# Attention backward: E and G of four key blocks in one tile and one DMA transpose, a four-pack PE step, and one exp unit more per block

## The chip, the cores and the metric

The kernel runs on one core of one Trainium2 chip. The metric is the device time of that core in microseconds (us). The engines are named as in the profile: PE (matrix multiplication), DVE (vector), ACT (activation), POOL, and SP, whose queue issues DMAs. Several runs of a kernel agree within 0.6% for the kernel before.

## The reference

The program is a transformer block and its gradients. Attention has 2048 positions, 32 heads, head size 16:

```
x = A_x;  xn = layernorm(x)
q, k, v = split(xn @ wqkv)                     # 32 heads of 16
p = softmax(q @ k^T * 0.25);  s = (p @ v) @ wo
g = silu(gelu(layernorm(xn) @ w1 + b1) @ w2 + b2)
out = x + s * g
# returned: out and the gradients for x, wqkv, wo, w1, b1, w2, b2
```

Only attention, forward and backward in one loop, changes. It takes some 1940 of 2629 us.

## The kernel before

Attention goes through 16 pairs of heads. A pair has four blocks of 512 queries, a block has 16 steps, one per key block of 128 keys. In step `g` the kernel

- computes scores `s` of the next step and exponentiates them on ACT into `et` (called E);
- computes `d` (the gradient of the probabilities, up to a factor) for two heads, and multiplies it by E on DVE into `gts` (called G);
- accumulates over the keys in `X`, with matmuls called L, E and G below (source: `Lc`, `NAT` with E, `NAT` with G);
- accumulates, for the block before, the gradients of K and V in `Z`. That needs E and G transposed. G is always transposed by DMA. E of half of the units is transposed by DMA (`ek`); for the other half it is computed again in the other orientation (`t`, then an exp into `e`).

The order of one step, and the transposes:

```python
    dma_units = tuple((kc, qb) for kc in range(4) for qb in (2, 3))
    ...
    etp = sb("etp", 3)      # E of four key blocks
    gtp = sb("gtp", 4)      # G of two key blocks
    gbp = sb("gbp", 5)      # G transposed
    ekp = sb("ekp", 5)      # E transposed
    ...                                                       # cut
        first = g % 16 == 1
        emit_t(g)                    # row packs: 32 rows x 128 columns of the PE array
        if not first:
            emit_le(g - 1)           # column packs: 128 rows x 32 columns
        emit_exp_b(g)
        emit_s(g + 1)                # row packs
        emit_d(g)                    # both heads at once, two PSUM buffers in all
        emit_mult(g)
        emit_exp_a(g + 1)
        emit_dmat(g)
        if first:
            emit_le(g - 1)
        emit_g(g - 1)                # column packs
        emit_z(g - lagb, 0)
        emit_z(g - lagb, 1)

    def emit_dmat(g):
        ...                                                   # cut
        if kb % 2 == 1:              # two transposes of G, 0.5 MB each, per group of four steps
            nc.sync.dma_start_transpose(out=blk[j]["Gk"][kc][:, h], in_=st_gt[g][:].rearrange("k a h q -> k (a h q)"))
        if kb % 4 == 3:              # and one of E, 0.5 MB
            nc.sync.dma_start_transpose(out=ek[:].rearrange("q b m k -> q (b m) k"), in_=st_et[g][:, 2:4].rearrange("k b a h q -> k (b a h q)"))
```

Matmuls on different rows, or on different columns, of the PE array run at the same time, four of them here (the timeline of PE below shows four on columns starting within 0.01 us; at 1200.85 us of the same kernel four on rows do so too): this is what "four-pack" means. On POOL a background task (the slope of gelu) runs along; its loads and stores, and the loads of the next pair's operands, are issued by SP as well.

## Time and profile before

| | before |
|---|---|
| time, median of the first 3 runs | 2628.93 us |
| attention | 282 to 2224 us of the span |
| one block, steady | 29.5 us |
| group of four steps, steady | 7.0 us |
| mean granted PE clock | 0.962 |

The first lines are from the page of the kernel before: busy time and share of the span by engine, the granted clock in 40 slices (tenths of full speed), and the chain of work that ended last, by engine and by line.

```profile
PE 2295.2 (87%) x18152; PEld 731.6 (28%) x18192; DVE 1837.6 (70%) x3286; ACT 1673.4 (64%) x1910; POOL 908.0 (35%) x1391
...
PEclk8899799999999999999999999999999999789999
...
PE 38%; DVE 33%; issue 12%; DMA 10%; ACT 4%; POOL 2%; SPq 0%; ACTq 0%; DVEq 0%; POOLq 0%
...
L743 DVE TENSOR_TENSOR gts<-d,et 128x512 bf16<-128x512 f32 x2048 | 1302.5, 682 | 359.1 <-issue 240.8
...
L708 PE MATMUL d<-QDT,KVT 32*128 32x512 bf16 x2048 | 599.1, 383 | 130.9 <-DVE gts L743 129.5
```

No engine is full, and `d` waits 129.5 us for DVE to finish with its buffers. The timeline of PE shows how (columns: start, duration, engine, line, operation, operands, count, and in brackets the idle time before and what ended it).

```profile
1171.99 0.38 PE L774 MATMUL X<-et,Lc 128*32 128x512 bf16 x2
1172.00 0.38 PE L858 MATMUL Z<-gk,W 128*32 128x512 bf16 x2
1172.22 0.38 PE L777 MATMUL X<-et,NAT 128*32 128x512 bf16 x2
1172.53 0.39 PE L694 MATMUL s<-QDT,KVT 32*128 32x512 bf16 x2
1172.71 0.37 PE L708 MATMUL d<-QDT,KVT 32*128 32x512 bf16 x1
1173.31 0.37 PE L708 MATMUL d<-QDT,KVT 32*128 32x512 bf16 x1 [0.23 <-DVE gts L743]
```

Four matmuls of one pack start within 0.01 us, packs of the same kind follow at 0.215 to 0.23 us, and a change between columns and rows costs a pitch of 0.32 us (1172.22 to 1172.53). The second `d` stands until the second gts of the step before has freed its buffer, and no other matmul starts in between (1172.71 to 1173.31).

The busy time by window gives the load of attention (columns: window, length, PE, weight loads, DVE, ACT, POOL with counts, granted clock, DMA share, GB/s).

```profile
300.00:2200.00 1900.00, 1750.78 (x15400) 472.20 (x15396) 1529.79 (x2592) 1479.56 (x1572) 764.74 (x1241) 0.99 1.17 233
```

### The profile page before, as it was taken

How to read it: one execution, taken by the hardware profiler on the slowest of the kernel's cores; microseconds unless marked ns; L12 is line 12 of the kernel's file. 1: busy time of each engine (PE TensorE's matmuls, PEld its weight loads, DVE VectorE, ACT ScalarE, POOL GpSimd, SP SyncE). 2: the span in 40 equal slices, each digit the busy share in tenths (PEclk: the TensorE clock that was granted, in tenths of full speed). 3: DMA queues.
4: the chain of work that ended last, by engine and by line, in shares of the span. 5: the costliest groups of instructions: out<-in, count | busy, mean ns of one | idle time of the engine just before them, and what ended most of it. 6: DMA issues, size and time to landing. Idle time of an engine off the chain costs nothing.

```text
span 2624.7 us, 47762 instructions
## 1 busy us (share of the span) xinstructions
PE 2295.2 (87%) x18152; PEld 731.6 (28%) x18192; DVE 1837.6 (70%) x3286; ACT 1673.4 (64%) x1910; POOL 908.0 (35%) x1391
## 2 busy tenths in 40 slices
PE   3788699999999999999999899999999997479998
PEld 2333122222222222222222222222222222134446
DVE  5766578887778878788878778888888885201652
ACT  3344578777777877788777777777777775011141
POOL 0533545454535445454445454521101111100020
PEclk8899799999999999999999999999999999789999
DMA  5355899999999999999999999999999998987475
GB/s 192 92 184 184 179 239 232 236 236 234 226 236 237 237 231 237 231 234 242 231 235 233 237 228 240 235 236 233 226 233 229 236 218 183 271 215 186 153 160 125
DMA packets 1905432, 568.51 MB, mean 217 GB/s; under 512 B 1811889, under 2 KB 1887794, under 8 KB 1905202
## 3 DMA queue, kind: packets, MB, share of 16 engines
q1 hardware_dynamic: 1844674, 511.05, 95.8%
q10 hardware_dynamic: 60528, 54.41, 6.7%
q8 instruction: 142, 2.33, 0.4%
q14 instruction: 88, 0.72, 0.1%
HBM read 52.83 MB, written 62.66 MB: 44 GB/s over the span
## 4 chain that ended last, share of the span: by engine, by line
PE 38%; DVE 33%; issue 12%; DMA 10%; ACT 4%; POOL 2%; SPq 0%; ACTq 0%; DVEq 0%; POOLq 0%
DVE gts L743 26%; PE d L708 6%; PE X L789 6%; PE Z L858 4%; DMA gk<-gts 4%; PE Z L852 3%; PE t L680 3%; PE X L774 2%; PE ps_dhg L463 2%; DVE xs L795 2%; ACT et L722 2%; DVE xt L807 2%; PE XT L805 1%; PE ps_dw L528 1%; PE ps_dw L442 1%
## 5 line engine op out<-in xcount | busy, mean ns | idle before, releaser
L743 DVE TENSOR_TENSOR gts<-d,et 128x512 bf16<-128x512 f32 x2048 | 1302.5, 682 | 359.1 <-issue 240.8
L722 ACT ACTIVATE et<-s 128x1024 bf16<-128x1024 f32 x1024 | 1002.6, 1024 | 24.9 <-PE d L708 13.8
L730 ACT ACTIVATE e<-t 128x1024 bf16<-128x1024 f32 x512 | 523.8, 1023 | 407.3 <-PE t L680 405.7
L708 PE MATMUL d<-QDT,KVT 32*128 32x512 bf16 x2048 | 599.1, 383 | 130.9 <-DVE gts L743 129.5
L694 PE MATMUL s<-QDT,KVT 32*128 32x512 bf16 x2048 | 403.3, 390 | 18.2 <-DMA QDT<-QDPad 11.9
L774 PE MATMUL X<-et,Lc 128*32 128x512 bf16 x2048 | 403.9, 391 | 14.1 <-DVE xs L795 14.1
L777 PE MATMUL X<-et,NAT 128*32 128x512 bf16 x2048 | 403.9, 391 | 0.0
L789 PE MATMUL X<-gts,NAT 128*17 128x512 bf16 x2048 | 402.5, 389 | 0.0
L858 PE MATMUL Z<-gk,W 128*32 128x512 bf16 x2048 | 399.4, 384 | 0.0
L822 POOL TENSOR_TENSOR W<-NATQd,rL 128x128 bf16<-128x128 bf16 x64 | 25.7, 402 | 645.9 <-DVE rL L817 645.9
L789 PEld LDWEIGHTS <-NAT 128*17 128x17 bf16 x2048 | 92.5, 87 | 492.0 <-issue 492.0
L852 PE MATMUL Z<-e,W 128*32 128x512 bf16 x1024 | 202.2, 388 | 3.8 <-DVE acc L865 2.3
L852 PE MATMUL Z<-ek,W 128*32 128x512 bf16 x1024 | 203.7, 394 | 0.0
L680 PE MATMUL t<-KVT,QDT 32*128 32x512 bf16 x1024 | 201.0, 389 | 0.0
L694 PEld LDWEIGHTS <-KVT 32*128 32x128 bf16 x2048 | 97.4, 91 | 362.6 <-issue 362.5
L708 PEld LDWEIGHTS <-KVT 32*128 32x128 bf16 x2048 | 139.0, 91 | 88.9 <-issue 59.6
L774 PEld LDWEIGHTS <-Lc 128*32 128x32 bf16 x2048 | 103.7, 93 | 180.4 <-issue 179.4
L865 DVE TENSOR_TENSOR acc<-Z,acc 64x512 f32<-64x512 f32 x192 | 129.2, 673 | 12.2 <-PE Z L858 12.2
L852 PEld LDWEIGHTS <-W 128*32 128x32 bf16 x2048 | 121.1, 93 | 56.7 <-issue 50.2
L777 PEld LDWEIGHTS <-NAT 128*32 128x32 bf16 x2048 | 101.2, 96 | 52.2 <-issue 2.7
L631 POOL TENSOR_TENSOR bg_v<-bg_t 128x512 f32<-128x512 f32 x56 | 58.1, 1038 | 149.1 <-ACT bg_t L638 149.1
L870 POOL CAST ob<-acc 64x512 bf16<-64x512 f32 x64 | 38.6, 603 | 203.3 <-DVE acc L865 203.3
(161 smaller groups left out, 2525.8 us busy)
## 6 DMA issues: line engine op xcount, KB each, us to landing
gk<-gts SPq DMA_TRANSPOSE x512, 4.1
HGT_s<-hgT SPq DMA_DIRECT2D x2, 3584.0 KB, 12.2
bg_x<-H1T_s SPq DMA_DIRECT2D x56, 128.0 KB, 2.8
GP_s<-bg_m SPq DMA_DIRECT2D x56, 128.0 KB, 2.5
gp<-GP_s ACTq DMA_DIRECT2D x8, 896.0 KB, 8.5
DH1T_s<-dh1T SPq DMA_DIRECT2D x4, 1792.0 KB, 10.2
NAT<-NAT_s SPq DMA_DIRECT2D x16, 264.0 KB, 3.2
GB_s<-gB ACTq DMA_DIRECT2D x16, 256.0 KB, 2.0
```

The costliest lines, as they stand in the source:

```text
L680: nc.tensor.matmul(t[:, hj, :], lhsT=op["QDT"][r:r + 32, q0:q0 + 128], rhs=op["KVT"][r:r + 32, kc * 512:(kc + 1) * 512], start=True, stop= ...
L694: nc.tensor.matmul(s[:, hj, :], lhsT=op["KVT"][r:r + 32, kb * 128:(kb + 1) * 128], rhs=op["QDT"][r:r + 32, qc * 512:(qc + 1) * 512], start ...
L708: nc.tensor.matmul(d[:], lhsT=op["KVT"][r:r + 32, kb * 128:(kb + 1) * 128], rhs=op["QDT"][r:r + 32, qc * 512:(qc + 1) * 512], start=True, ...
L722: nc.scalar.activation(out=et[:, :, kb % 4, :, :].rearrange("k b h q -> k h b q"), in_=st_s.pop(g)[:].rearrange("k h (b q) -> k h b q", b= ...
L730: nc.scalar.activation(out=e[:], in_=st_t.pop(g)[:], func=ACT.Exp)
L743: nc.vector.tensor_tensor(out=gts[:, kb % 2, hj, :].rearrange("k (b q) -> k b q", b=4), in0=ds[hj][:].rearrange("k (b q) -> k b q", b=4), ...
L774: nc.tensor.matmul(X[64 + 32 * hj:96 + 32 * hj, :], lhsT=Lc[:], rhs=et[:, :, kb % 4, hj, :], start=(kb == 0), stop=False, skip_group_check ...
L777: nc.tensor.matmul(X[32 * hj:32 * hj + 32, :], lhsT=NATt[:, kb, hj, 1:33], rhs=et[:, :, kb % 4, hj, :], start=(kb == 0), stop=(kb == 15), ...
L789: nc.tensor.matmul(X[64 + 32 * hj:64 + 32 * hj + 17, :], lhsT=NATt[:, kb, hj, 0:17], rhs=gts[:, kb % 2, hj, :], start=False, stop=(kb == 1 ...
L852: nc.tensor.matmul(Z[32 * hj:32 * hj + 32, :], lhsT=blk[j]["W1"][:, qb, hj, :], rhs=ev[:, hj], start=(qb == qb_order[0]), stop=False, tile ...
L858: nc.tensor.matmul(Z[32 * hj:32 * hj + 32, :], lhsT=blk[j]["W2"][:, qb, hj, :], rhs=gv[:, :, :, hj, qb, :], start=False, stop=(qb == qb_or ...
L865: nc.vector.tensor_tensor(out=av, in0=Z[0:64, :], in1=av, op=ALU.add)
```

## The change

Its intent: take PE out from behind DVE by issuing the two `d` of a step half a step apart; fill every pack to three or four matmuls; let SP issue one large transpose per group instead of three; move plain DMAs from SP to ACT; and relieve DMA by computing one more unit of E again (the exp unit: `t` and `e`), so that the first group of a block moves 1.25 MB instead of 1.5. `xs` moves from DVE to ACT.

```diff
-    dma_units = tuple((kc, qb) for kc in range(4) for qb in (2, 3))
+    n_moved = (1, 2, 2, 2)
+    dma_units = tuple((kc, qb) for kc in range(4) for qb in range(4 - n_moved[kc], 4))
@@ pools
-    etp = sb("etp", 3)
-    gtp = sb("gtp", 4)
-    gbp = sb("gbp", 5)
-    ekp = sb("ekp", 5)
-    ep = sb("ep", lagb + 2)
+    egp = sb("egp", 3)
+    tgp = sb("tgp", 5)
+    ep = sb("ep", 4)
@@ operand loads; the two transfers of the gelu slope likewise
-            nc.sync.dma_start(out=t["NAT"][:]...
+            nc.scalar.dma_start(out=t["NAT"][:]...
@@ emit_exp_a: one tile for E and G
+            eg = egp.tile([128, 8192], bf16, name="eg")
@@ emit_dmat, once per four steps
+        n = n_moved[kc]
+        tg = tgp.tile([128, 48, 128], bf16, name="tg")
+        nc.sync.dma_start_transpose(out=tg[:, 0:8 * n + 32, :], in_=st_et[g][0][:, (4 - n) * 1024:8192])
@@ emit_zg: odd units go to the upper half of Z, so two units make a four-pack
+            c = 32 * hj + 64 * (i % 2)
@@ the step
+        emit_s(g + 1)
+        emit_d(g, 0)
+        if not first:
+            emit_l(g - 1)
+        if i == 0:
+            emit_e(g - 1)
+        else:
+            emit_ze(gz)
+            if i % 2 == 1:
+                emit_zg(gz - 1)
+                emit_zg(gz)
+        emit_d(g, 1)
+        emit_t(g)
         ...                                                  # cut: exps, mult, acc, dmat
+        if i != 0:
+            emit_e(g - 1)
         emit_g(g - 1)
+        if i == 0:
+            emit_ze(gz)
```

(The copies for the operands share one padded tile; `acc` has 128 partitions, and its upper half is added on POOL at the end of a pair.)

More of the change, by code (lines that the diff above doesn't have):

```diff
@@ L569, in attention_core @@
         ))
-    KVPad = opnd.tile([128, 16, 4, 32], bf16, name="KVPad")
-    QDPad = opnd.tile([128, 16, 4, 32], bf16, name="QDPad")
-    nc.gpsimd.memset(KVPad[:], 0.0)
-    nc.gpsimd.memset(QDPad[:], 0.0)
+    Pad = opnd.tile([128, 16, 4, 32], bf16, name="Pad")
+    nc.gpsimd.memset(Pad[:], 0.0)
     Lc = opnd.tile([128, 32], bf16, name="Lc")
@@ L577, in attention_core @@
     opnd.tile([128, 192], mybir.dt.uint8, name="pad_to_256b")
-    acc = opnd.tile([64, S], f32, name="acc")
+    acc = opnd.tile([128, S], f32, name="acc")
     def load_ops(p):
@@ L583, in plain @@
         def plain():
-            nc.sync.dma_start(out=t["NAT"][:].rearrange("q k j c -> q k (j c)"), in_=NAT_s[p])
-            nc.sync.dma_start(out=t["NATQq"][:].rearrange("q k j c -> q k (j c)"), in_=NATQ_s[0][p])
-            nc.sync.dma_start(out=t["NATQd"][:].rearrange("q k j c -> q k (j c)"), in_=NATQ_s[1][p])
+            nc.scalar.dma_start(out=t["NAT"][:].rearrange("q k j c -> q k (j c)"), in_=NAT_s[p])
+            nc.scalar.dma_start(out=t["NATQq"][:].rearrange("q k j c -> q k (j c)"), in_=NATQ_s[0][p])
+            nc.scalar.dma_start(out=t["NATQd"][:].rearrange("q k j c -> q k (j c)"), in_=NATQ_s[1][p])
         def ck():
-            nc.gpsimd.tensor_copy(out=KVPad[:, :, 0:2, 0:17], in_=t["NAT"][:, :, :, 0:17])
-            nc.gpsimd.tensor_copy(out=KVPad[:, :, 2:4, 0:16], in_=t["NAT"][:, :, :, 17:33])
+            nc.gpsimd.tensor_copy(out=Pad[:, :, 0:2, 0:17], in_=t["NAT"][:, :, :, 0:17])
+            nc.gpsimd.tensor_copy(out=Pad[:, :, 2:4, 0:16], in_=t["NAT"][:, :, :, 17:33])
         def tk():
             nc.sync.dma_start_transpose(out=t["KVT"][:].rearrange("r (m k) -> r m k", m=16),
-                                        in_=KVPad[:].rearrange("q m j c -> q (m j c)"))
+                                        in_=Pad[:].rearrange("q m j c -> q (m j c)"))
         def cq():
-            nc.gpsimd.tensor_copy(out=QDPad[:, :, 0:2, 0:17], in_=t["NATQq"][:])
-            nc.gpsimd.tensor_copy(out=QDPad[:, :, 2:4, 0:16], in_=t["NATQd"][:])
+            nc.gpsimd.tensor_copy(out=Pad[:, :, 0:2, 0:17], in_=t["NATQq"][:])
+            nc.gpsimd.tensor_copy(out=Pad[:, :, 2:4, 0:16], in_=t["NATQd"][:])
         def tq():
             nc.sync.dma_start_transpose(out=t["QDT"][:].rearrange("r (m k) -> r m k", m=16),
-                                        in_=QDPad[:].rearrange("q m j c -> q (m j c)"))
-        return [plain, ck, cq, tk, tq]
+                                        in_=Pad[:].rearrange("q m j c -> q (m j c)"))
+        return [plain, ck, tk, cq, tq]
     blocks = [(p, qc) for p in range(npairs) for qc in range(nqc)]
@@ L607, in attention_core @@
     NSTEP = NB * 16
-    st_s, st_t, st_d, st_et, st_e, st_gt = {}, {}, {}, {}, {}, {}
+    st_s, st_t, st_d, st_et, st_e = {}, {}, {}, {}, {}
     blk = [dict(Gk={}, Ek={}) for _ in range(NB)]
@@ L614, in attention_core @@
     GC = float(np.sqrt(2.0 / np.pi))
+    n_slope = 4 * FC
     def gelu_slope_ops():
@@ L619, in load @@
             x = bgp.tile([128, 512], bf16, name="bg_x")
-            nc.sync.dma_start(out=x[:], in_=H1T_s[fc * 128:(fc + 1) * 128, sc * 512:(sc + 1) * 512])
+            nc.scalar.dma_start(out=x[:], in_=H1T_s[fc * 128:(fc + 1) * 128, sc * 512:(sc + 1) * 512])
             return x
@@ L623, in gelu_slope_ops @@
         yield
-        for i in range(4 * FC):
+        for i in range(n_slope):
             sc, fc = divmod(i, FC)
@@ L641, in gelu_slope_ops @@
             tt(m, m, x)
-            if i + 1 < 4 * FC:
+            if i + 1 < n_slope:
                 nx = load(i + 1)
@@ L654, in gelu_slope_ops @@
             yield
-            nc.sync.dma_start(out=GP_s[fc * 128:(fc + 1) * 128, sc * 512:(sc + 1) * 512], in_=m[:])
+            yield
+            nc.scalar.dma_start(out=GP_s[fc * 128:(fc + 1) * 128, sc * 512:(sc + 1) * 512], in_=m[:])
             yield
@@ L695, in emit_s, with emit_d @@
                              start=True, stop=True, tile_position=(r, 0))
-    def emit_d(g):
+    def emit_d(g, hj):
         a = a_unit(g)
@@ L703, in emit_d @@
         qc = blocks[j][1]
-        ds = []
-        for hj in range(2):
-            r = 64 + 32 * hj
-            d = ps_d.tile([128, 512], f32, name="d", tag="d")
-            nc.tensor.matmul(d[:], lhsT=op["KVT"][r:r + 32, kb * 128:(kb + 1) * 128], rhs=op["QDT"][r:r + 32, qc * 512:(qc + 1) * 512],
-                             start=True, stop=True, tile_position=(r, 0))
-            ds.append(d)
-        st_d[g] = ds
+        r = 64 + 32 * hj
+        d = ps_d.tile([128, 512], f32, name="d", tag="d")
+        nc.tensor.matmul(d[:], lhsT=op["KVT"][r:r + 32, kb * 128:(kb + 1) * 128], rhs=op["QDT"][r:r + 32, qc * 512:(qc + 1) * 512],
+                         start=True, stop=True, tile_position=(r, 0))
+        st_d.setdefault(g, []).append(d)
     def emit_exp_a(g):
@@ L718, in emit_exp_a @@
         if kb % 4 == 0:
-            cur["et"] = etp.tile([128, 4, 4, 2, 128], bf16, name="et")
-        et = cur["et"]
-        st_et[g] = et
-        nc.scalar.activation(out=et[:, :, kb % 4, :, :].rearrange("k b h q -> k h b q"),
+            eg = egp.tile([128, 8192], bf16, name="eg")
+            cur["eg"] = (eg, eg[:, 0:4096].rearrange("k (b a h q) -> k b a h q", b=4, a=4, h=2),
+                         eg[:, 4096:8192].rearrange("k (a h q) -> k a h q", a=4, h=2))
+        st_et[g] = cur["eg"]
+        nc.scalar.activation(out=cur["eg"][1][:, :, kb % 4, :, :].rearrange("k b h q -> k h b q"),
                              in_=st_s.pop(g)[:].rearrange("k h (b q) -> k h b q", b=4), func=ACT.Exp)
@@ L736, in emit_mult @@
         kb = a[1]
-        if kb % 2 == 0:
-            cur["gts"] = gtp.tile([128, 2, 2, 512], bf16, name="gts")
-        gts = cur["gts"]
-        st_gt[g] = gts
+        _, et, gts = st_et[g]
         ds = st_d.pop(g)
         for hj in range(2):
-            nc.vector.tensor_tensor(out=gts[:, kb % 2, hj, :].rearrange("k (b q) -> k b q", b=4), in0=ds[hj][:].rearrange("k (b q) -> k b q", b=4),
-                                    in1=st_et[g][:, :, kb % 4, hj, :], op=ALU.mult)
+            nc.vector.tensor_tensor(out=gts[:, kb % 4, hj, :].rearrange("k (b q) -> k b q", b=4), in0=ds[hj][:].rearrange("k (b q) -> k b q", b=4),
+                                    in1=et[:, :, kb % 4, hj, :], op=ALU.mult)
     def emit_dmat(g):
         a = a_unit(g)
-        if a is None:
+        if a is None or a[1] % 4 != 3:
             return
@@ L751, in emit_dmat, with emit_l @@
         kc = kb // 4
-        if kb % 2 == 1:
-            h = (kb // 2) % 2
-            if h == 0:
-                blk[j]["Gk"][kc] = gbp.tile([128, 2, 16, 128], bf16, name="gk")
-            nc.sync.dma_start_transpose(out=blk[j]["Gk"][kc][:, h], in_=st_gt[g][:].rearrange("k a h q -> k (a h q)"))
-        if kb % 4 == 3:
-            ek = ekp.tile([128, 2, 8, 128], bf16, name="ek")
-            for qb in (2, 3):
-                blk[j]["Ek"][(kc, qb)] = ek[:, qb - 2]
-            nc.sync.dma_start_transpose(out=ek[:].rearrange("q b m k -> q (b m) k"), in_=st_et[g][:, 2:4].rearrange("k b a h q -> k (b a h q)"))
-    def emit_le(g):
+        n = n_moved[kc]
+        tg = tgp.tile([128, 48, 128], bf16, name="tg")
+        nc.sync.dma_start_transpose(out=tg[:, 0:8 * n + 32, :], in_=st_et[g][0][:, (4 - n) * 1024:8192])
+        for i in range(n):
+            blk[j]["Ek"][(kc, 4 - n + i)] = tg[:, 8 * i:8 * i + 8]
+        blk[j]["Gk"][kc] = tg[:, 8 * n:8 * n + 32]
+    def emit_l(g):
         a = a_unit(g)
@@ L770, in emit_le @@
         X = blk[j]["X"]
-        NATt = op_of(j)["NAT"]
-        et = st_et[g]
+        et = st_et[g][1]
         for hj in range(2):
@@ L775, in emit_le, with emit_e @@
                              start=(kb == 0), stop=False, skip_group_check=True, tile_position=(0, 64 + 32 * hj))
+    def emit_e(g):
+        a = a_unit(g)
+        if a is None:
+            return
+        j, kb = a
+        X = blk[j]["X"]
+        NATt = op_of(j)["NAT"]
+        et = st_et[g][1]
         for hj in range(2):
@@ L786, in emit_g @@
         NATt = op_of(j)["NAT"]
-        gts = st_gt[g]
+        gts = st_et[g][2]
         for hj in range(2):
-            nc.tensor.matmul(X[64 + 32 * hj:64 + 32 * hj + 17, :], lhsT=NATt[:, kb, hj, 0:17], rhs=gts[:, kb % 2, hj, :],
+            nc.tensor.matmul(X[64 + 32 * hj:64 + 32 * hj + 17, :], lhsT=NATt[:, kb, hj, 0:17], rhs=gts[:, kb % 4, hj, :],
                              start=False, stop=(kb == 15), skip_group_check=True, tile_position=(0, 64 + 32 * hj))
         st_et.pop(g)
-        st_gt.pop(g)
         if kb == 15:
             xs = xsp.tile([128, 512], f32, name="xs")
-            nc.vector.tensor_copy(out=xs[:], in_=X[:])
+            nc.scalar.copy(out=xs[:], in_=X[:])
             blk[j]["xs"] = xs
@@ L805, in emit_finalize @@
             nc.tensor.transpose(XT[:, qb, :], xs[:, qb * 128:(qb + 1) * 128], ident_f32[:])
-        xt = finp.tile([128, 4, 128], f32, name="xt")
+        xt = finp.tile([128, 4, 128], f32, name="xt", bufs=1)
         nc.vector.tensor_copy(out=xt[:], in_=XT[:])
@@ L835, in emit_finalize, with z_unit @@
         blk[j]["W2"] = W2
-    def emit_z(g, part):
+    def z_unit(g):
         b = b_unit(g)
         if b is None:
-            return
-        j, kc, qb = b
-        p, qc = blocks[j]
-        if part == 0:
-            if qb == qb_order[0]:
-                cur["Z"] = ps_z.tile([64, 512], f32, name="Z", tag="z")
-            Z = cur["Z"]
-            if (kc, qb) in dma_units:
-                ev = blk[j]["Ek"].pop((kc, qb)).rearrange("q (a h) k -> q h a k", h=2)
-            else:
-                ev = st_e.pop(g)[:].rearrange("q h (a k) -> q h a k", a=4)
-            for hj in range(2):
-                nc.tensor.matmul(Z[32 * hj:32 * hj + 32, :], lhsT=blk[j]["W1"][:, qb, hj, :], rhs=ev[:, hj],
-                                 start=(qb == qb_order[0]), stop=False, tile_position=(0, 32 * hj))
-            return
-        Z = cur["Z"]
-        gv = blk[j]["Gk"][kc][:].rearrange("q a (r h b) k -> q a r h b k", r=2, h=2)
-        for hj in range(2):
-            nc.tensor.matmul(Z[32 * hj:32 * hj + 32, :], lhsT=blk[j]["W2"][:, qb, hj, :], rhs=gv[:, :, :, hj, qb, :],
-                             start=False, stop=(qb == qb_order[3]), tile_position=(0, 32 * hj))
-        if qb == qb_order[3]:
-            av = acc[:, kc * 512:(kc + 1) * 512]
-            if qc == 0:
-                nc.vector.tensor_copy(out=av, in_=Z[0:64, :])
-            else:
-                nc.vector.tensor_tensor(out=av, in0=Z[0:64, :], in1=av, op=ALU.add)
-            if qc == nqc - 1:
-                if kc == 0:
-                    cur["ob"] = outp.tile([64, S], bf16, name="ob")
-                ob = cur["ob"]
-                nc.gpsimd.tensor_copy(out=ob[:, kc * 512:(kc + 1) * 512], in_=av)
-                if kc == 3:
-                    for hj in range(2):
-                        for kv in range(2):
-                            late.append((g + lagb + 2, lambda hj=hj, kv=kv: nc.sync.dma_start(
-                                out=dKVT_out[(1 - kv) * D + p * 32 + hj * 16:(1 - kv) * D + p * 32 + hj * 16 + 16, :],
-                                in_=ob[hj * 32 + kv * 16:hj * 32 + kv * 16 + 16, :])))
@@ new lines, in z_unit, with emit_ze @@
+            return None
+        return b + (g % 4,)
+    def emit_ze(g):
+        u = z_unit(g)
+        if u is None:
+            return
+        j, kc, qb, i = u
+        if i == 0:
+            cur["Z"] = ps_z.tile([128, 512], f32, name="Z", tag="z")
+        Z = cur["Z"]
+        if (kc, qb) in dma_units:
+            ev = blk[j]["Ek"].pop((kc, qb)).rearrange("q (a h) k -> q h a k", h=2)
+        else:
+            ev = st_e.pop(g)[:].rearrange("q h (a k) -> q h a k", a=4)
+        for hj in range(2):
+            nc.tensor.matmul(Z[32 * hj:32 * hj + 32, :], lhsT=blk[j]["W1"][:, qb, hj, :], rhs=ev[:, hj],
+                             start=(i == 0), stop=False, tile_position=(0, 32 * hj), skip_group_check=True)
@@ new lines, in emit_zg, with emit_acc @@
+    def emit_zg(g):
+        u = z_unit(g)
+        if u is None:
+            return
+        j, kc, qb, i = u
+        Z = cur["Z"]
+        gv = blk[j]["Gk"][kc].rearrange("q (a h b) k -> q a h b k", a=4, h=2)
+        for hj in range(2):
+            c = 32 * hj + 64 * (i % 2)
+            nc.tensor.matmul(Z[c:c + 32, :], lhsT=blk[j]["W2"][:, qb, hj, :], rhs=gv[:, :, hj, qb, :],
+                             start=(i == 1), stop=(i >= 2), tile_position=(0, c), skip_group_check=True)
+    def emit_acc(g):
+        u = z_unit(g)
+        if u is None or u[3] != 3:
+            return
+        j, kc, qb, i = u
+        p, qc = blocks[j]
+        Z = cur["Z"]
+        av = acc[:, kc * 512:(kc + 1) * 512]
+        if qc == 0:
+            nc.vector.tensor_copy(out=av, in_=Z[:])
+        else:
+            nc.vector.tensor_tensor(out=av, in0=Z[:], in1=av, op=ALU.add)
+        if qc == nqc - 1:
+            if kc == 0:
+                cur["ob"] = outp.tile([64, S], bf16, name="ob")
+            ob = cur["ob"]
+            hi = outp.tile([64, 512], f32, name="hi")
+            nc.gpsimd.tensor_copy(out=hi[:], in_=acc[64:128, kc * 512:(kc + 1) * 512])
+            nc.gpsimd.tensor_tensor(out=ob[:, kc * 512:(kc + 1) * 512], in0=acc[0:64, kc * 512:(kc + 1) * 512],
+                                    in1=hi[:], op=ALU.add)
+            if kc == 3:
+                for hj in range(2):
+                    for kv in range(2):
+                        late.append((g + lagb + 2, lambda hj=hj, kv=kv: nc.sync.dma_start(
+                            out=dKVT_out[(1 - kv) * D + p * 32 + hj * 16:(1 - kv) * D + p * 32 + hj * 16 + 16, :],
+                            in_=ob[hj * 32 + kv * 16:hj * 32 + kv * 16 + 16, :])))
@@ L894, in attention_core @@
         first = g % 16 == 1
+        gz = g - lagb
+        i = gz % 4
+        emit_s(g + 1)
[4 more added lines that the diff above has]
+            emit_e(g - 1)
+        else:
+            emit_ze(gz)
[3 more added lines that the diff above has]
+        emit_d(g, 1)
         emit_t(g)
-        if not first:
-            emit_le(g - 1)
+        emit_exp_a(g + 1)
         emit_exp_b(g)
-        emit_s(g + 1)
-        emit_d(g)
         emit_mult(g)
-        emit_exp_a(g + 1)
+        emit_acc(gz)
         emit_dmat(g)
         if first:
-            emit_le(g - 1)
+            emit_l(g - 1)
+        if i != 0:
+            emit_e(g - 1)
         emit_g(g - 1)
-        emit_z(g - lagb, 0)
-        emit_z(g - lagb, 1)
+        if i == 0:
+            emit_ze(gz)
         if g >= 17 and (g - 17) % 16 == 0 and (g - 17) // 16 < NB:
```

## The prediction

> **What bounds it now.** Attention, about 281 to 2224 us, is most of the span; only it changes. There (busy time by window) PE is busy 92%, DVE 81%, ACT 78%: nothing is full. The timeline shows a fixed rhythm of 7.0 us per four steps, 29.5 us per block of 16 (xs copy to xs copy). It is a PE-DVE loop. Both d matmuls of a step are issued together into two buffers. Every second step PE waits for the second gts to free its buffer (d at 1202.12, next d at 1202.71), then for acc before Z (1203.02, then 1203.30). DVE meanwhile idles 0.57 to 0.85 us. The chain of waits agrees: PE 38%, DVE 33%, gts alone 26%. Without those waits PE needs about 5.2 us per four steps.
>
> DMA is not the bound: binning the packets gives a plateau of 290 GB/s, the mean is 234.[...]
>
> **What changes, with durations of the trace.**
> - PE: same packs of matmuls (4.5 per step, 0.215 us each), but four row/column changes per step instead of three. A change makes the pitch 0.32 instead of 0.215[...]. Cost: 0.05 us per step. In return d is split: head 0 at the step's start, head 1 half a step later with t, so PE no longer stands behind two gts; Z's first write moves to the end of its step, after acc.
> - DVE: loses xs (0.68 us per block). gts (pitch 0.605) and acc stay.
> - ACT: one exp more (pitch 0.92), xs (about 0.6), 2.5 DMA issues per block (0.33 to 0.8 us elsewhere in this trace, partly hidden). About 24 to 25 us per block.
> - DMA: 5.75 instead of 6 MB per block, one issue instead of three. At 290 GB/s about 22 us per block with the rest. A 1.5 MB transpose lands about 7.5 us after issue (estimate); its eg buffer is wanted about 10.5 us after: tight, not binding.
>
> **On the critical path.** I walked the new order by hand with these durations and the two-buffer rings of s/t and d (on the old order the walk gives 3.35 and 3.64 us per two steps, as the timeline shows). Ordinary group: 6.06 us (was 7.0). First group of a block, with the extra exp, xs, transposes of X and finalize: about 8.2. Block: 3 x 6.06 + 8.2 = 26.4; tanh, DMA issues on ACT and jitter make it about 27.0. Saving 2.5 us x 64 = 160 us.
>
> **Predicted: 2470 us, 80% range 2405 to 2555.** Faster by over 2%: 0.89; within 2%: 0.08; slower: 0.03.
>
> **Right or wrong in the profile.** Right: four steps take 6.0 to 6.3 us; d waits for gts mostly gone; PE idle shrinks; ACT and DVE both 87 to 92% busy in attention; DMA mean about 250 GB/s; chain shifts from gts towards et and e. Wrong: et or gts waiting on tg (DMA), long ACT issue times, or d still waiting for gts in most steps.
>
> **What would break it.** The single late transpose may miss its buffer's reuse, so that ACT waits once per group (back towards 2550 or above).[...] d1 and t may not overlap as assumed. The block's first group, with the exp and xs now on the fullest engine, may cost more than 8.2 us.

The sum: a block of 3 x 6.06 + 8.2 = 26.4 us, about 27.0 with what is added, 2.5 us less in each of 64 blocks, 160 us less than 2630, so 2470 us. The 7.5 us for a 1.5 MB transpose: the trace of the kernel before gives about as much, 7.7 us: 4.1 to landing for 0.5 MB and 3.6 for another 1 MB at 290 GB/s (an estimate from these two).

## The result and the profile after

| | before | changed |
|---|---|---|
| median (range), 4 runs each | 2629.94 us (2627.68 to 2637.29) | 2565.49 us (2552.27 to 2573.38) |
| ratio, 95% interval | | 0.9745 (0.9699 to 0.9792) |
| mean granted PE clock of the profiled run | 0.962 | 0.891 |
| steady group of four steps at full clock | 7.0 us | 6.02 us |
| block wholly at full clock, median | 29.55 us (55 of 63) | 26.27 us (33 of 63) |
| time at half clock between first and last step | 64 us | 433 us |

Blocks are counted from the first `s` of a block to that of the next. The trace records the granted clock as stretches at full or at half speed; the last two rows combine those with the steps.

The page of the changed kernel, in the same order as above:

```profile
PE 2324.2 (90%) x18320; PEld 744.8 (29%) x18320; DVE 1853.6 (72%) x3222; ACT 1773.9 (69%) x2038; POOL 990.2 (39%) x1454
...
PEclk8899569888999979699998988698997998889999
...
PE 62%; DMA 15%; ACT 8%; DVE 6%; POOL 3%; SPq 3%; issue 2%; ACTq 1%; DVEq 0%; POOLq 0%
...
L738 DVE TENSOR_TENSOR eg<-d,eg 128x512 bf16<-128x512 f32 x2048 | 1349.4, 687 | 249.4 <-PE d L706 77.6
...
L706 PE MATMUL d<-QDT,KVT 32*128 32x512 bf16 x2048 | 857.4, 419 | 8.8 <-DVE eg L738 8.3
...
L764 PE MATMUL X<-eg,Lc 128*32 128x512 bf16 x2048 | 439.6, 426 | 3.8
```

The wait of `d` for DVE is gone: 129.5 us became 8.3 us. But the mean of one matmul rose (`d` from 383 to 419 ns), and the clock row, all nines in attention before but for its start, now shows many slices of 5 to 8. PE is busier because its matmuls are slower. PE's share of the chain rises from 38% to 62%, in part for the same reason (in E12, where the clock is held, it is 51%) and in part because DVE has left the chain.

Two windows of the changed kernel, 16 and 36 us long, make it plain:

```profile
1180.00:1196.00 16.00, 15.38 (x148) 4.13 (x145) 14.26 (x23) 13.20 (x14) 10.09 (x16) 1.00 1.18 248
910.00:946.00 36.00, 36.00 (x227) 7.07 (x225) 22.49 (x34) 24.40 (x26) 13.49 (x17) 0.50 0.98 212
```

In the second PE is busy 36.00 of 36.00 us and does 6.3 matmuls per us; in the first it is busy 96% and does 9.3. At half clock a step takes 2.47 us (mean of 157), at full clock 1.65 (mean of 828). So 433 us at half clock cost about 433 x (1 - 1.65 / 2.47) = 144 us, an estimate from the trace. Without them the profiled run would be near 2430 us. The repeats point the same way: the four runs had granted clocks of 0.891, 0.895, 0.899 and 0.907, and took 2573.38, 2568.42, 2562.55 and 2552.27 us, in that order. From the first to the last the clock means about 86 us less at half clock (561 to 474 us of the whole span) and the time is 21 us shorter, 0.24 us for each, somewhat less than the third that the estimate takes (E11's fastest and slowest run below: 269 and 78 us, 0.29).

What starts such a stretch? Here is the timeline at 903 us, the second block of a pair, where ACT issues the operand loads (three lines of ACT, then PE):

```profile
903.23 2.22 ACTq L582 DMA_DIRECT2D NATQq<-NATQq_s  x1
...
905.48 1.05 ACTq L583 DMA_DIRECT2D NATQd<-NATQd_s  x1
...
906.58 1.02 ACT L720 ACTIVATE eg<-s 128x1024 bf16<-128x1024 f32 x1 [2.48 <-issue]
...
907.65 0.39 PE L694 MATMUL s<-QDT,KVT 32*128 32x512 bf16 x2 [2.31 <-ACT eg L720]
...
909.48 0.59 PE L694 MATMUL s<-QDT,KVT 32*128 32x512 bf16 x2 [0.20 <-ACT eg L720]
```

ACT stands 2.22 and 1.05 us in issuing; the next exp starts 2.48 us late; PE pauses 2.31 us; and 1.8 us later each matmul takes 0.59 us instead of 0.39. This stretch at half clock lasts 37.5 us, to step 3 of the next block. Why these two issues take so long is not shown. SP is issuing a transpose at the same time, but that alone does not do it: of the 112 issues for the gelu slope on ACT, 99 lie wholly within an issue of SP, and all 112 took 0.33 to 0.37 us. Only the second and the third of three loads in a row took long, and not in every pair. The other kind of start has a late transpose behind it:

```profile
836.27 1.03 ACT L728 ACTIVATE e<-t 128x1024 bf16<-128x1024 f32 x1
838.82 1.94 ACT L720 ACTIVATE eg<-s 128x1024 bf16<-128x1024 f32 x2 [1.52 <-DMA tg<-eg]
```

Here ACT waits 1.52 us to write E, until DMA has read the `eg` tile. In all, 19 stretches at half clock lie between the first blocks and the end of attention, each begins 0.9 to 4.2 us after the start of a PE pause of 0.55 to 2.64 us (the one just shown has 0.55), and seven are over 20 us long. One pause, of 1.64 us at 1260.5 us, has no stretch behind it.

The trace was then cut into the windows of 3.413 us in which the clock changes (every stretch is a multiple of that), from the first step to the last. For each window I took the share of the time in which at least one matmul streams, counting for each the pitch that matmuls of its kind have in this trace when they follow each other: 216 ns for one of 512 columns at full clock (L442, 182 of 221) and 427 at half (L409, 14 of 24), and for one of the 128-column transposes `XT` (L803) 109 and 213; this is an estimate from the pitches.

| window of the changed kernel, attention | number | streaming share, lowest / median / highest |
|---|---|---|
| full clock, stays full | 398 | 0.47 / 0.72 / 0.77 |
| full clock, next is half | 19 | 0.13 / 0.44 / 0.55 |
| half clock, stays half | 106 | 0.54 / 0.80 / 0.84 |
| half clock, next is full | 20 | 0.80 / 0.83 / 0.86 |

In this trace no window with a share above 0.56 came before a fall; between 0.47 and 0.56 some did and some did not. A window before a return is denser in the median (0.83 against 0.80), but the two ranges overlap from 0.80 to 0.84, so this share does not tell when the clock comes back. What can be said: at half clock the new step's windows are about 0.80 full, since each of its four row/column changes takes a pitch of 0.54 us (940.25 to 940.79 us), of which the count takes 0.427 as streaming; it stays at half clock although in 101 of the 106 windows the profile shows under 0.1 us of PE idle; and all seven stretches over 20 us end at step 3 or 4 of the next block, where `XT` and more `t` are.

The kernel before is a useful contrast. It too has 14 PE pauses over 0.8 us in attention after its first block (19 us in sum; the changed kernel has 20, 31 us). Eight stretches at half clock follow after its first blocks, but they last 3.4 to 13.7 us, 41 us in all; the 19 of the changed kernel last 3.4 to 44.4 us, 355 us in all. So the loss is less in the number of pauses than in how long the new order then stays at half clock. Which property of the order does it was not isolated.

### The profile page after: what moved, and what is told of

It reads as the page before. It is cut to its first block, busy times and chain, and to the rows that moved or that the text cites. A ratio compares the mean times of both kernels' runs of the same rounds, so it can differ in the third digit from the quotient of the medians.

```text
span 2571.6 us, 47302 instructions
## 1 busy us (share of the span) xinstructions
PE 2324.2 (90%) x18320; PEld 744.8 (29%) x18320; DVE 1853.6 (72%) x3222; ACT 1773.9 (69%) x2038; POOL 990.2 (39%) x1454
## 4 chain that ended last, share of the span: by engine, by line
PE 62%; DMA 15%; ACT 8%; DVE 6%; POOL 3%; SPq 3%; issue 2%; ACTq 1%; DVEq 0%; POOLq 0%
PE d L706 12%; PE X L764 11%; PE s L694 10%; DMA tg<-eg 9%; PE X L776 7%; PE Z L866 4%; ACT eg L720 3%; PE X L788 3%; ACT e L728 2%; PE ps_dhg L463 2%; PE Z L854 2%; PE ps_h L212 1%; PE ps_dw L442 1%; PE XT L803 1%; PE ps_dw L528 1%
## 5 line engine op out<-in xcount | busy, mean ns | idle before, releaser
L738 DVE TENSOR_TENSOR eg<-d,eg 128x512 bf16<-128x512 f32 x2048 | 1349.4, 687 | 249.4 <-PE d L706 77.6
L720 ACT ACTIVATE eg<-s 128x1024 bf16<-128x1024 f32 x1024 | 1033.2, 1027 | 208.8 <-PE d L706 114.4
L706 PE MATMUL d<-QDT,KVT 32*128 32x512 bf16 x2048 | 857.4, 419 | 8.8 <-DVE eg L738 8.3
L728 ACT ACTIVATE e<-t 128x1024 bf16<-128x1024 f32 x576 | 593.4, 1030 | 79.6 <-PE t L680 78.7
L764 PE MATMUL X<-eg,Lc 128*32 128x512 bf16 x2048 | 439.6, 426 | 3.8
L776 PE MATMUL X<-eg,NAT 128*32 128x512 bf16 x2048 | 440.2, 427 | 0.0
L788 PE MATMUL X<-eg,NAT 128*17 128x512 bf16 x2048 | 434.2, 420 | 0.0
L706 PEld LDWEIGHTS <-KVT 32*128 32x128 bf16 x2048 | 187.9, 92 | 382.1 <-issue 382.1
L866 PE MATMUL Z<-tg,W 128*32 128x512 bf16 x2048 | 222.2, 417 | 0.0
L694 PEld LDWEIGHTS <-KVT 32*128 32x128 bf16 x2048 | 108.1, 92 | 308.7 <-issue 308.0
L854 PE MATMUL Z<-tg,W 128*32 128x512 bf16 x896 | 191.1, 423 | 0.0
L880 DVE TENSOR_TENSOR acc<-Z,acc 128x512 f32<-128x512 f32 x192 | 130.5, 680 | 9.2 <-PE Z L866 9.2
```

What stands on the lines that cost most here:

```text
L694: nc.tensor.matmul(s[:, hj, :], lhsT=op["KVT"][r:r + 32, kb * 128:(kb + 1) * 128], rhs=op["QDT"][r:r + 32, qc * 512:(qc + 1) * 512], start ...
L706: nc.tensor.matmul(d[:], lhsT=op["KVT"][r:r + 32, kb * 128:(kb + 1) * 128], rhs=op["QDT"][r:r + 32, qc * 512:(qc + 1) * 512], start=True, ...
L720: nc.scalar.activation(out=cur["eg"][1][:, :, kb % 4, :, :].rearrange("k b h q -> k h b q"), in_=st_s.pop(g)[:].rearrange("k h (b q) -> k ...
L728: nc.scalar.activation(out=e[:], in_=st_t.pop(g)[:], func=ACT.Exp)
L738: nc.vector.tensor_tensor(out=gts[:, kb % 4, hj, :].rearrange("k (b q) -> k b q", b=4), in0=ds[hj][:].rearrange("k (b q) -> k b q", b=4), ...
L764: nc.tensor.matmul(X[64 + 32 * hj:96 + 32 * hj, :], lhsT=Lc[:], rhs=et[:, :, kb % 4, hj, :], start=(kb == 0), stop=False, skip_group_check ...
```

## The experiments

Two theories stood. CLOCK: the loop is as fast as predicted, and what is missing against the prediction is time at half clock, started by PE pauses and (the part that stays argued) held by the step's own gaps. QUEUE: the waiting itself, for transposes and for DMA issue, is the loss, and the clock is a side effect. A third name, SUPPLY, was added in the second round for the question where the pauses come from: SP and DMA need nearly all of a block's time. All results were correct. Times are medians of four runs, ratios against the runs of the kernel before in the same rounds. "Pauses" are PE idle times over 0.8 us in attention after its first block; "half" is time at half clock between the first and the last step; both are of the profiled run.

### E1: the order of the step alone

```diff
 # the changed kernel, with E and G in tiles of their own (etp 3, gtp 4, gbp 5, ekp 5),
 # three 0.5 MB transposes per group as before, all plain DMAs on SP, and
-    n_moved = (1, 2, 2, 2)
+    n_moved = (2, 2, 2, 2)
```

> One part alone: the new order of the PE step (with xs on ACT and Z in two halves), but E and G in tiles of their own, three 0.5 MB transposes per group, all plain DMAs on SP and no extra exp, as before. Theory CLOCK (the new order removes the d-waits-for-gts loop; what was lost against the prediction is half-clock time started by PE pauses): groups of four steps at full clock still near 6.0 us, blocks wholly at full clock near 26; SP has more to issue (about 25.5 us of transposes and plain DMAs per block), so pauses and half-clock stretches at least as many as in the change's run (433 us); time 2520 to 2600. Rival QUEUE (the gain comes from the merged transposes and the freed SP queue): time close to before, 2600 to 2640.

Measured: 2685.3 us, ratio 1.0204 (1.0175 to 1.0233). Half 644 us, pauses 29, blocks wholly at full clock 26.25 us in the median, but only 18 of 63. The block time is as CLOCK had it; the total is worse than either theory allowed. The new order alone makes the kernel slower than before: it asks for a transpose group every 6 us, the supply cannot follow (gts waits for a transpose to free its buffer 65 times, 97 us in all, against 17 times and 30 us before), and pauses and half clock eat more than the order gains.

### E2: the rest without the order of the step

```diff
 # the changed kernel, with the step in the old order:
+        emit_t(g)
+        if not first:
+            emit_l(g - 1)
+            emit_e(g - 1)
+        emit_exp_b(g)
+        emit_s(g + 1)
+        emit_d(g, 0)
+        emit_d(g, 1)
+        emit_mult(g)
+        emit_exp_a(g + 1)
+        emit_dmat(g)
         ...                          # G, Z with E, Z with G, acc, as before
```

> The other part alone: one merged transpose per group, plain DMAs on ACT, the extra exp, xs on ACT, but the old order of the step. CLOCK: the old rhythm of 7.0 us per ordinary group stays, blocks 29 to 30.5 us, half-clock time within 20 to 150 us[...]; time 2610 to 2660. QUEUE: 2540 to 2590.

Measured: 2606.66 us, ratio 0.9890 (0.9868 to 0.9911). Half 57 us, pauses 4, blocks at full clock 29.44 us. The old rhythm is there as expected; the time is 3 us below the range given, with fewer disturbed blocks than before (58 of 63 are wholly at full clock, against 55). So neither part alone brings the gain. The order makes a faster loop, the merged transposes feed it.

### E3: operand loads back on SP

```diff
-            nc.scalar.dma_start(out=t["NAT"][:]...      # and NATQq, NATQd
+            nc.sync.dma_start(out=t["NAT"][:]...
```

> The change with only the three operand loads of each head pair back on SP. In the change's run ACT stood up to 2.3 us in issuing them (1.84 us for one), and PE paused 1.5 to 2.3 us at step 3 of the second block of a pair, where five of the stretches of 37 to 41 us at half clock begin. CLOCK: those pauses and those stretches go, half-clock time falls from 433 to 150 to 280 us, time 2495 to 2535; pauses in the third block of a pair (late transposes) stay or grow a little. QUEUE: only the 2 us per pair come back, at most 32 us: 2530 to 2555, half-clock time then explains nothing.

Measured: 2526.52 us, ratio 0.9592 (0.9537 to 0.9646). Half 268 us. No stretch begins at step 3 of the second block of a pair any more (in the changed kernel four did, after pauses of 2.12 to 2.64 us). Three DMA issues per pair, 48 in all, on the wrong engine cost some 39 us (2565.49 to 2526.52, two sets of rounds). By the intervals of the two ratios that is 20 to 60 us, so the time alone does not rule out the 32 us that QUEUE allowed at most; the 165 us less at half clock speak for CLOCK. Pauses are still 19, now mostly of the late-transpose kind.

### E4: bursts of empty matmuls, with a flaw

```diff
+    Zc = opnd.tile([128, 32], bf16, name="Zc")           # zeros
+    nc.gpsimd.memset(Zc[:], 0.0)
     Lc = opnd.tile([128, 32], bf16, name="Lc")
@@ before emit_g(g - 1)
+        if g % 16 == 8 and (g // 16) % 4 in (1, 2):
+            for r in range(6):                           # adds zero to X
+                nc.tensor.matmul(X[96:128, :], lhsT=Zc[:], rhs=et[:, :, kb % 4, 1, :], start=False, stop=False, ...)
```

> The change with six extra matmuls with zero weights, adding zero into X, in a row at step 8 of the second and third block of each pair (32 bursts; at most 1.3 us each at full clock, 41 us in all). In the change's run a stretch at half clock ended only at steps 1 to 4 of the next block[...]. CLOCK: stretches that begin in steps 1 to 7 of those blocks now end at step 8 to 10; none of 30 us or more that spans step 8 of such a block is left; half-clock time falls from 433 to 200 to 300 us; time 2520 to 2570 in spite of the added work. QUEUE: the added work simply adds: 2580 to 2605, half-clock stretches as long as before.

Measured: 2778.59 us, ratio 1.0556. This says nothing about the bursts: every block was slower, also those without one, and a transpose took 7.34 us in the median instead of 6.12. The tile of zeros is 64 bytes per partition and had moved every later tile by 64 bytes. That is 20% more time for the same bytes; with the tiles where they were, E5 has 6.14 us again. Why the offset costs time is not shown.

### E5: the same bursts, nothing moved

```diff
-    opnd.tile([128, 192], mybir.dt.uint8, name="pad_to_256b")
+    opnd.tile([128, 128], mybir.dt.uint8, name="pad_to_256b")
```

> The last run again with its flaw mended: its 64-byte tile of zeros had moved every later tile by 64 bytes, and the transposes took 7.34 us each instead of 6.12. Now the zeros lie in the padding and nothing moves. CLOCK: transposes 6.1 us again; half-clock stretches that reach step 8 of the second or third block of a pair end at steps 8 to 10; at most one stretch of over 30 us is left (7 over 20 us in the change's run); half-clock time 200 to 320 us; time 2515 to 2570 in spite of up to 41 us of added work. QUEUE: 2575 to 2605 and stretches as long as before.

Measured: 2530.51 us, ratio 0.9610 (0.9573 to 0.9646). Half 180 us, transposes 6.14 us, pauses 15. Half is below the range given. PE got 192 matmuls more, the blocks that hold them take 27.5 to 30.9 us at full clock (median 28.0) instead of 26.3, and the kernel is 35 us faster. Each of the seven stretches that reach a burst ends within 4 us of its first matmul; here is one, begun 17 us earlier at a pause:

```profile
567.71 0.64 PE L877 MATMUL Z<-tg,W 128*32 128x512 bf16 x4
568.29 0.60 PE L708 MATMUL d<-QDT,KVT 32*128 32x512 bf16 x1
568.29 0.60 PE L682 MATMUL t<-KVT,QDT 32*128 32x512 bf16 x2
568.82 0.61 PE L778 MATMUL X<-eg,NAT 128*32 128x512 bf16 x2
568.83 1.46 PE L787 MATMUL X<-eg,Zc 128*32 128x512 bf16 x3
569.66 0.60 PE L799 MATMUL X<-eg,NAT 128*17 128x512 bf16 x1
570.09 1.49 PE L787 MATMUL X<-eg,Zc 128*32 128x512 bf16 x3
...
572.42 0.39 PE L766 MATMUL X<-eg,Lc 128*32 128x512 bf16 x2
```

Before the burst a matmul takes 0.60 to 0.64 us, after it 0.39. QUEUE expected the added work simply to add, 2580 us or more; it falls. That the half clock is the loss (433 us became 180), and that a dense run of matmuls ends it (seven stretches of seven), is shown by this run. That the step's own gaps are what holds it fits, but is argued: what makes the clock fall or come back is not shown.

### E6: operands spread over the pair

```diff
 # on E3: copies and transposes of the next pair's operands at steps 5, 13, 21, 33 instead of 5, 9, 13, 17
-        return [plain, ck, tk, cq, tq]
+        return [(1, plain), (5, ck), (13, tk), (21, cq), (33, tq)]
```

> Operand loads back on SP, and the copies and transposes of the next pair's operands spread over the second, third and fourth block (steps 5, 13, 21, 33 after its start instead of 5, 9, 13, 17), so that SP's extra 6.5 us per pair do not fall into one stretch. The bytes stay. SUPPLY (SP and DMA need about 25.4 us of each 26.3 us block: a burst makes the merged transposes late, ACT waits for its eg tile, PE pauses, the clock halves): PE pauses over 0.8 us fall from 19 to 8 or fewer, half-clock time from 268 to under 130 us (some 35 of it at the start), time 2450 to 2490. If the pauses came from something else than SP's bursts: unchanged, 2510 to 2545.

Measured: 2515.25 us (2490.46 to 2521.03), ratio 0.9535 (0.9485 to 0.9584). Half 270 us, pauses 13. A miss, and not clear of E3 by the intervals. It does not rule out the bursts of SP, though: in the trace each of the 13 pauses that remain has, in the 20 us before it, either an operand transpose (5) or the loads and stores at the turn of a pair, which were not spread (8).

### E7: one exp unit more, 5.5 MB per block

```diff
 # on E3
-    n_moved = (1, 2, 2, 2)
+    n_moved = (1, 2, 1, 2)
```

> Operand loads back on SP and one exp unit more (the third group of a block moves 1.25 MB too): SP needs 1 us less per block, ACT 0.92 us more. SUPPLY: lateness and pauses fall, half-clock time under 150 us; a block at full clock grows by 0.3 to 0.6 us (26.6 to 26.9); time 2460 to 2510. If ACT were the engine that pauses PE: blocks 27.2 or more, time 2530 to 2570.

Measured: 2511.21 us (2485.17 to 2539.19), ratio 0.9573 (0.9517 to 0.9628). The last run counts as slow, but this ratio cannot be reached without it: even 2511.61, the slowest of the others, over 2630.77, the fastest before, is only 0.955. Half 108 us, pauses 6, blocks at full clock 27.09 us; time and block are a bit above the ranges given. The profile is of the fastest run (granted clock 0.951; the others had 0.940, 0.939 and 0.922), so half and pauses are those of a lucky one. Less to transpose means fewer pauses, as SUPPLY says, but a block at full clock is 0.8 us longer, in time the gain on E3 is not clear of the scatter, and the scatter shows that a few pauses by chance still decide over 20 to 50 us.

### E8: three issues instead of one

```diff
 # on E3
-        nc.sync.dma_start_transpose(out=tg[:, 0:8 * n + 32, :], in_=eg[:, (4 - n) * 1024:8192])
+        for lo, hi in ((0, 8 * n), (8 * n, 8 * n + 16), (8 * n + 16, 8 * n + 32)):
+            nc.sync.dma_start_transpose(out=tg[:, lo:hi, :], in_=eg[:, c0 + lo * 128:c0 + hi * 128])
```

> Operand loads back on SP; each merged transpose issued as three (E part, two halves of G) one after the other at the same place, into the same tile. SUPPLY: the rate is set by the bytes, 1.97 us per 0.5 MB in the kernel before against 6.12 per 1.5 MB, so SP's issue time changes by under 3% and the time stays within 2505 to 2550 (as with the loads on SP alone, 2527). MERGING (one large transfer is itself better): transposes take longer in sum, pauses grow, 2560 to 2620.

Measured: 2586.30 us, ratio 0.9821 (0.9792 to 0.9851), against 2526.52 in one piece. SP's time for these transposes rose from 1562 to 1621 us, 3.8%. Half 392 us, pauses 23. The expectation of MERGING holds: one issue is better than three. It is a small saving that counts much, because the supply is so close to the demand (26.2 us of SP's time for a block of 26.3 in the changed kernel).

### E9: 5.5 MB and spread operands together

```diff
 # E3 + E6 + E7
```

> Candidate for the best version: operand loads on SP, 5.5 MB per block (one exp unit more), operand copies and transposes spread over three blocks. SUPPLY: SP's issue time about 1600 of 1770 us as in the run with 5.5 MB, its bursts flattened: at most 4 PE pauses over 0.8 us, half-clock time under 90 us, time 2475 to 2500, repeats within 15 us of each other. If spreading does nothing: like the run with 5.5 MB alone, 2485 to 2540.

Measured: 2483.03 us (2480.94 to 2494.33), ratio 0.9442 (0.9406 to 0.9479). No pause over 0.8 us. Half 119 us, of which 68 are in the first two blocks; the expectation of under 90 was missed for that reason. The other 51 us are five stretches that begin at pauses of 0.44 to 0.79 us, so shorter pauses do it too. The repeats lie within 14 us. The granted clocks of the four runs are 0.945 to 0.952, against 0.922 to 0.951 in E7. So spreading, which did little at 5.75 MB, does its part once there is room (the two sets of times overlap in one run).

### E10: loads and stores on POOL

```diff
 # on E7, without the move of the loads to SP
-            nc.scalar.dma_start(out=t["NAT"][:]...       # and NATQq, NATQd; the dKVT stores likewise
+            nc.gpsimd.dma_start(out=t["NAT"][:]...
```

> 5.5 MB per block, and both the operand loads and the dKVT stores issued by POOL, so that SP issues transposes alone and ACT only the two gelu-slope transfers. SP's issue time falls by about 50 us against the run with 5.5 MB and loads on SP. SUPPLY: 2470 to 2500, half-clock time under 90 us. If POOL's issuing holds up W1 and W2 or the copies for the operands, PE pauses at Z instead: 2510 to 2600.

Measured: 2504.96 us (2498.84 to 2514.58), ratio 0.9514 (0.9481 to 0.9548). Half 120 us, pauses 5; SP's issue time fell by 37 us against E7 (1599 to 1562). The expectation (2500 us at most, half under 90) was missed. Not better than E7 beyond the scatter, and worse than E9. The trace shows what remains: four of the five pauses, of 2.96 to 2.98 us, come when POOL issues the four stores in a row (2.02 us), ACT's tanh of the gelu slope waits 2.43 us for POOL, and the exp stands behind it.

### E11: no extra exp unit, 6 MB per block

```diff
 # on E3
-    n_moved = (1, 2, 2, 2)
+    n_moved = (2, 2, 2, 2)
```

> Operand loads on SP and no extra exp: 6 MB per block again, all groups 1.5 MB; ACT has 0.92 us less and SP 1 us more per block, about 26.3 of the 26.0 us that a block would need at full clock. SUPPLY: transposes fall behind, PE pauses 30 or more (19 with 5.75 MB, 6 with 5.5), half-clock time over 350 us, time 2560 to 2640. If ACT's load were what matters: 2470 to 2520.

Measured: 2606.37 us (2598.53 to 2676.96; the last counts as slow and is out of the ratio), ratio 0.9886 (0.9853 to 0.9920). Half 490 us, pauses 21, fewer than expected; blocks at full clock 26.27 us. With 6, 5.75 and 5.5 MB per block the medians are 2606, 2527 and 2511 us, and half 490, 268 and 108 us, while the block at full clock stays or grows (26.27, 26.27, 27.09). ACT was given more work each time, and the kernel did not become slower: the bytes matter, not ACT. The step from 6 to 5.75 MB is clear in time; the one from 5.75 to 5.5 is not in E3 and E7, but is just so with spread operands (E6 and E9: 0.9485 to 0.9584 against 0.9406 to 0.9479).

### E12: the best version, with two bursts at the start

```diff
 # E9 + the burst of E5, but only twice
+        if g in (4, 20):
+            emit_kick(g - 1, 6)      # six matmuls with zero weights, adding zero to X
```

> The best version so far (5.5 MB per block, loads on SP, spread operands), with two bursts of six zero matmuls, one at step 4 of block 0 and one at step 4 of block 1. Attention starts at half clock; in the best version's profile 67 of its 119 us at half clock lie in the first two blocks (33.9 and 36.6 us long, against 27.0). CLOCK: the bursts end the first stretch within a few steps, half-clock time in the first two blocks falls from 67 to 10 to 30 us, time 2455 to 2482. If the burst does not lift the clock there: 2480 to 2496.

Measured: 2454.76 us (2450.95 to 2459.02), ratio 0.9320 (0.9288 to 0.9352). Half in the first two blocks fell from 68 to 16 us, in all from 119 to 30 us; the first two blocks take 28.3 and 27.0 us instead of 33.9 and 36.6. Twelve matmuls that compute nothing save 28 us. This version beats both kernels, and its clock row is again like that of before:

```profile
PE 2192.0 (90%) x18420; PEld 754.5 (31%) x18460; DVE 1840.7 (75%) x3222; ACT 1813.3 (74%) x2102; POOL 989.6 (40%) x1455
...
PEclk8899799999999999999999999999999998889999
```

PE has more matmuls than in the changed kernel and is busy 132 us less.

## Why the prediction was wrong

The direction was right and the loop was right; the time was outside the range by 10 us, and 95 us above the estimate. Point by point:

- **"Ordinary group: 6.06 us", "Block: 3 x 6.06 + 8.2 = 26.4."** Right. The trace has 6.02 us for a group (Z with G at 1182.63 and again at 1188.65), 26.27 us for the median block wholly at full clock. Walking the order by hand with durations from the trace was accurate to 1%.
- **"d waits for gts mostly gone."** Right, 129.5 to 8.3 us. E2 shows that without the new order the block stays at 29.44 us.
- **"At 290 GB/s about 22 us per block with the rest."** This step failed: the term was too small. 290 GB/s is a rate that the packets reach in bins of 0.2 to 1 us; over bins of 5 us the median is 244 (changed kernel, 600 to 1600 us). A whole transpose of 1.5 MB takes 6.22 us of SP's time in the median, 253 GB/s, and SP issued for 1677 us in attention, that is 26.2 us for each of 64 blocks where a block at full clock takes 26.3. The prediction had the better number before it and took a peak instead: in the trace of the kernel before, a transpose takes 1.97 us per 0.5 MB, 266 GB/s, and SP issued for 1794 us, 28.0 us of each 29.55 us block.
- **"Lands about 7.5 us after issue ... wanted about 10.5 us after: tight, not binding."** It landed 8.8 us after issue in the median (9.1 for those of 1.5 MB) and up to 13.0, and ACT waited for it 30 times, 39.2 us in all. So the wait that was called not binding was binding. E11, E3 and E7 have ever fewer pauses with fewer bytes, E9 none over 0.8 us. The lines of the changed kernel's `tg`, and of `gk` before (durations in ns: lowest, median, highest; those of `tg` mix 1.25 and 1.5 MB):

```profile
L749 SPq DMA_TRANSPOSE tg<-eg x256: 4867/6113/10874, 294.5 to 2151.5; - x128
...
  ACT eg L720: 39.2, 30
...
DMA to landing us min/median/max: 6.4/8.8/13.0
```

```profile
L756 SPq DMA_TRANSPOSE gk<-gts x512: 1316/1966/4403, 287.7 to 2204.7; - x171
...
DMA to landing us min/median/max: 3.6/4.1/6.4
```

- **"2.5 DMA issues per block (0.33 to 0.8 us elsewhere in this trace, partly hidden)"** priced them at almost nothing, though "long ACT issue times" stood among the signs of being wrong; the 0.33 to 0.8 us leave out longer issues on ACT in the kernel before, outside attention, of up to 2.57 us. Long issues happened about once in three pairs (up to 2.22 us for one), and E3 shows what they cost: about 39 us. What makes them long is not shown.
- **What was missing altogether: the clock.** The prediction took the granted clock of before as a constant. The pauses alone are worth little: 20 of them over 0.8 us sum to 31 us. The 433 us at half clock are worth about 144 us by the estimate above; E5 shows that the loss is there and not in the waits, since work added to PE made the kernel faster. With the clock held, E12 ends at 2454.76 us, below the prediction of 2470.
- **"ACT and DVE both 87 to 92% busy", "DMA mean about 250 GB/s", "chain shifts towards et and e."** Not in the changed kernel, whose window of 300 to 2150 us has ACT at 86%, DVE at 84%, 231 GB/s:

```profile
300.00:2150.00 1850.00, 1787.59 (x15579) 487.48 (x15582) 1550.21 (x2537) 1582.70 (x1703) 845.63 (x1303) 0.89 1.13 231
```

The gain that was expected was thus made and most of it given back: 63 blocks at the mean of its undisturbed ones (26.51 us) would take 1670 us, they took 1837; before, they took 1891. Of 221 us, 54 were kept.

What stays open: what makes the clock fall and come back, and so which property of the step, if any, decides whether it recovers by itself. E2 and the kernel before, which have three row/column changes per step, show no stretch over 14 us after their first blocks; E2 has few pauses, but the kernel before has 14 and recovers from each. And why some of the three loads take so long to issue on ACT.

## What to carry to other kernels

When a change makes a loop tighter, ask what rate its slowest supplier sustains over a whole transfer, not what it reaches at its peak, and leave some per cent of room: here 8% fewer bytes than before, at the price of two more exp units per block, was better than an evenly loaded schedule. Look at the granted clock before reading any busy share: a PE at 100% may be a PE at half speed (36.00 of 36.00 us busy at a clock of 0.50 above), and a pause of 2.4 us can cost another 15 (an estimate: 44.4 us at half clock, of which a third is lost). If a loop cannot climb back by itself, a few dense matmuls that compute nothing, put where the pause is known to be, can be worth more than they cost (in E12 twelve saved 28 us).
